# A chunked attention feeding a mixture of experts: the dense network moved wholly into the attention loop, and expert slots of 128 neighbouring rows

## The chip, the cores and the metric

The kernel runs on one core of a Trainium2 chip. The core has a matrix engine (PE, whose weight loads are listed as PEld), a vector engine (DVE), an activation engine (ACT), a general engine (POOL) and a sync engine (SP, which only issues transfers). All of them share 16 DMA engines. The metric is the device time of one execution in microseconds, lower being better.

## The reference, cut to what matters

```python
# attention: B, H, S, D = 4, 8, 768, 64; chunks of 32 queries that see 16 keys
# to the left, their own 32, 8 to the right, and 8 memory keys
for c in range(S // 32):
    k_full = np.concatenate([mem_k, k[:, :, l_start:r_end]], axis=2)
    v_full = np.concatenate([mem_v, v[:, :, l_start:r_end]], axis=2)
    a = softmax(np.matmul(q_c, k_full.transpose(0, 1, 3, 2)) / sqrt(D))
    out[:, :, c_start:c_end] = np.matmul(a, v_full)
x = out.transpose(0, 2, 1, 3).reshape(3072, 512)

# one dense network and eight experts, 512 -> 512 -> 512
y_dense = np.maximum(x @ w1_dense, 0.0) @ w2_dense
logits = x @ w_gate
expert_idx = np.argmax(logits, axis=1)
gate_w = softmax(logits)[np.arange(N), expert_idx]
for e in range(8):
    mask = expert_idx == e
    y_moe[mask] = gate_w[mask, None] * (np.maximum(x[mask] @ w1[e], 0.0) @ w2[e])
return y_dense + y_moe
```

Every token goes through the dense network and through one expert, chosen by its logits. Which expert gets how many tokens is known only when all logits are there.

## The kernel before

The 3072 tokens are 24 tiles of 128. The work has two stages, and the order of the instructions on each engine is the order in which the program is written.

**Attention loop.** It has 29 turns, counted by `i`. In one turn different tiles are at different steps: tile `i` has its scores made, tile `i-1` is transposed (`turn`), tile `i-2` is multiplied with the values and normalised, tile `i-3` becomes the network's input (`keep_x`, `turn_x`), tile `i-4` goes through the gate. Every third turn a group of three tiles gets its experts and its rows in the sorted array (`choose`, `rank`, `place`). A tile's row is then written by an indirect DMA (`scatter`, seven turns behind) to `xs` in DRAM, where each expert has a region of its own. A row of `xs` is 514 words: 256 words of the token's input as bf16, 256 words of the dense hidden layer as bf16, the sum of the exponentials of its logits, and its token number.

Keys and queries of the next batch are transposed on PE during the loop (`transposes`, one `step` for the keys or for the queries of two heads). A turn runs one step at its head, and in some turns a second one at its end; `steps_at` says how many. A key step is followed by two copies on ACT, a query step by one.

The first layer of the dense network (`dense`) comes seven turns behind: four matmuls with the tile as stationary operand and 512 hidden units as moving ones, into the one PSUM buffer of pool `pf`, and an activation on ACT that scales the result by the sum of exponentials and puts it into the row.

**Tables.** After the last turn DVE works out, for each of up to 31 slots, its expert (`expi`) and, for each of its 128 lanes, which row of `xs` to fetch (`rowi`). A lane without a token fetches a row of zeros.

**Slots.** A slot is up to 128 tokens of one expert. `fetch` gathers its rows by an indirect DMA on POOL. `turn` transposes input and dense hidden layer on PE, and DVE and ACT copy them out of PSUM. `bring` reads the expert's number into a register of DVE and copies that expert's two weight matrices to a fixed place. `first` is the first layer, with a relu on ACT. `second` adds the dense second layer and the expert's second layer in one PSUM buffer. `send` divides by the sum on ACT, and an indirect DMA on POOL writes the rows to the output. For the tokens of this input 27 slots suffice; slots 27 to 30 stand behind a branch on the number of slots (`tc.If(count > NSURE)`), placed before the last seven slots, and `run` gives the order around it.

All weights are cast to bf16 on the way in by DMAs that POOL issues (`load_w`); `next_w` issues one more at the turns of `W_AT`, the last ones during the first slots.

Of the kernel before, what the change touches and what calls it, by code (L numbers as in the profile page):

```python
# [17 lines left out]
ENGINES = [mybir.EngineType.PE, mybir.EngineType.DVE, mybir.EngineType.Activation]  # L18
# [7 lines left out]
NT = B * TPB  # L26
# [10 lines left out]
NSURE = 27  # L37
NSPLIT = 20
XW = DM // 2
ROW = 2 * XW + 2  # L40
ZROW = E * CAP
NOWHERE = 1 << 20
GRP = 3
QKB = 5
NVB = 4
W_AT = (10, 13, 15, 16, 18, 19, 21, 22, 24, 25, 26, 27)
NXG = 5
# [3 lines left out]
def kernel(  # L51
# [19 lines left out]
    xs = nc.dram_tensor("xs", [E * CAP + 1, ROW], I32, kind="Internal").ap()  # L71
# [14 lines left out]
    w_todo = [(E, 1)] + [(e, half) for e in range(E) for half in range(2)]  # L86
# [12 lines left out]
    zrow = const.tile([1, ROW], F32, name="zrow")  # L99
    rowi = const.tile([128, NSLOT], I32, name="rowi")  # L100
    expi = const.tile([128, NSLOT], I32, name="expi")
    nsl = const.tile([128, 1], I32, name="nsl")
# [8 lines left out]
    def constants():  # L111
        nc.vector.memset(ones, 1.0)
        nc.vector.memset(oh_sum, 0.0)
        nc.vector.memset(zrow, 0.0)
        nc.vector.memset(zrow[:, ROW - 2:ROW - 1], 1.0)
        nc.vector.memset(zrow[:, ROW - 1:ROW].bitcast(I32), NOWHERE)
        nc.sync.dma_start(xs[ZROW:ZROW + 1, :], zrow.bitcast(I32))
        for e in range(E):
            nc.gpsimd.memset(prio[:, e:e + 1], float(E - e))
            nc.gpsimd.memset(ecap[:, :, e:e + 1], float(e * CAP // 128))  # L120
        nc.gpsimd.iota(tok, [[128, NT]], base=0, channel_multiplier=1)
        nc.gpsimd.affine_select(upper, ones, pattern=[[1, 128]], base=0,
                                channel_multiplier=-1, compare_op=ALU.is_gt, fill=0.0)

    def table_constants():
        nc.gpsimd.iota(thr_i, [[128, NT]], base=0, channel_multiplier=0)
        nc.gpsimd.iota(lane_i, [[0, 1]], base=0, channel_multiplier=1)
        nc.gpsimd.iota(slot_i, [[1, NSLOT]], base=0, channel_multiplier=0)
# [7 lines left out]
    with ExitStack() as one:  # L136
# [138 lines left out]
        def attention(g, qT, kbd):  # L275
# [68 lines left out]
            def turn_x():  # L344
# [5 lines left out]
                xT = work.tile([128, DT, 128], BF16, tag="xT", name="xT", bufs=5)  # L350
# [9 lines left out]
            def dense():  # L360
                ph = pf.tile([128, F], F32, tag="ph", name="ph")
                for d in range(DT):
                    nc.tensor.matmul(ph, st["xT"][:, d, :], wall[:, E, d, :],  # L363
                                     start=(d == 0), stop=(d == DT - 1))
                nc.scalar.activation(st["row"][:, XW:2 * XW].bitcast(BF16), ph, AF.Relu,
                                     scale=st["grp"]["gt"][:, st["u"], 0:1])

            return {"scores": scores, "exp": expo, "turn": turn, "values": values, "norm": norm,
                    "keep_x": keep_x, "turn_x": turn_x, "gate": gate, "dense": dense}

        scatters = []
# [48 lines left out]
        def scatter(g):  # L420
# [5 lines left out]
                row.bitcast(I32), None, bounds_check=E * CAP - 1, oob_is_err=False)  # L426
            for o in scatters:
                tc.declare_no_dep(i.ins, o.ins, reason="different rows of xs")
# [27 lines left out]
        LAG_X, LAG_G, LAG_D = 3, 4, 7  # L456
        for i in range(NT + LAG_G + 1):
# [24 lines left out]
            if i == 2:  # L482
                load_w(E, 0)
                table_constants()
            if i in W_AT:
                next_w()
            if i % 2 == 0:
                load_v(i // 2 + 2)
# [25 lines left out]
            do("norm", 2)  # L514
            do("exp", 0)
# [13 lines left out]
            if i >= LAG_D:  # L529
                scatter(i - LAG_D)  # L530
        for g in range(NT + LAG_G + 1 - LAG_D, NT):
# [19 lines left out]
        nc.vector.tensor_copy(nsl, pin[:, E - 1:E])  # L551
# [9 lines left out]
        nc.vector.tensor_tensor(done, sw, ew(pin), ALU.is_ge)  # L561
        ex = tmp([128, NSLOT], "exq")
        nc.vector.reduce_sum(ex, done, axis=AX.X)
        nc.vector.tensor_scalar(expi, ex, float(E - 1), None, ALU.min)
        mine = wide_t[0][:, NSLOT * E:2 * NSLOT * E].rearrange("p (s e) -> p s e", e=E)
        nc.vector.tensor_tensor(mine, sw, ew(pex), ALU.is_ge)
# [7 lines left out]

        fr = tmp([128, NSLOT], "fr")
        nc.vector.tensor_tensor(fr, slot, st, ALU.subtract)
        nc.vector.tensor_scalar(fr, fr, 128.0, lane, op0=ALU.mult, op1=ALU.add)
        ok = tmp([128, NSLOT], "ok")
        nc.vector.tensor_tensor(ok, ce, fr, ALU.is_gt)
        nc.vector.scalar_tensor_tensor(fr, ex, float(CAP), fr, op0=ALU.mult, op1=ALU.add)  # L580
        nc.vector.scalar_tensor_tensor(fr, fr, float(-ZROW), ok, op0=ALU.add, op1=ALU.mult)
        nc.vector.tensor_scalar(rowi, fr, float(ZROW), None, ALU.add)

    with ExitStack() as two:
# [5 lines left out]
        xgs, xts, hs, copied = {}, {}, {}, {}  # L590
        own = [""]
        sent = []

        def fetch(j):
            xg = w3.tile([128, ROW], F32, tag="xg" + own[0], name="xg", bufs=NXG)
            nc.gpsimd.indirect_dma_start(  # L596
                xg.bitcast(I32), None, xs[:, :],
                bass.IndirectOffsetOnAxis(ap=rowi[:, j:j + 1], axis=0),
                bounds_check=ZROW, oob_is_err=True)
            xgs[j] = xg  # L600

        def turn(j):
            xb = xgs[j][:, :2 * XW].bitcast(BF16)
            xt = pt.tile([128, DT + FT, 128], BF16, tag="xt", name="xt")
            for d in range(DT + FT):
                nc.tensor.transpose(xt[:, d, :], xb[:, 128 * d:128 * d + 128], ident)  # L606
            xT = w3.tile([128, DT + FT, 128], BF16, tag="xT" + own[0], name="xT", bufs=2)
            nc.vector.tensor_copy(xT[:, :DT], xt[:, :DT])  # L608
            nc.scalar.copy(xT[:, DT:], xt[:, DT:])  # L609
            xts[j] = xT  # L610

        def bring(j):
            n = min(j + 1, E)
            ev = nc.vector.value_load(expi[:1, j:j + 1], min_val=0, max_val=n - 1)
            wa = w2.tile([128, DT, 512], BF16, tag="wa" + own[0], name="wa")
            wb = w2.tile([128, FT, 512], BF16, tag="wb" + own[0], name="wb")
            nc.vector.tensor_copy(  # L617
                wa, wall[:, :n][:, bass.ds(ev, 1), :DT].rearrange("p a t m -> p (a t) m"))
            nc.vector.tensor_copy(
                wb, wall[:, :n][:, bass.ds(ev, 1), DT:].rearrange("p a t m -> p (a t) m"))  # L620
            copied[j] = (wa, wb)

        def first(j):
            w, xT = copied[j][0], xts[j]
# [5 lines left out]
            h = w2.tile([128, FT, 128], BF16, tag="h", name="h")  # L630
# [3 lines left out]
        def second(j, dense):  # L634
            if dense:
                hs[j, "py"] = pf.tile([128, DM], F32, tag="py", name="py")
            py = hs[j, "py"]
            for f in range(FT):
                if dense:
                    nc.tensor.matmul(py, xts[j][:, DT + f, :], wall[:, E, DT + f, :],  # L640
                                     start=(f == 0), stop=False)
                else:
                    nc.tensor.matmul(py, hs[j][:, f, :], copied[j][1][:, f, :],  # L643
                                     start=False, stop=(f == FT - 1))

        def send(j, o=None, then=True):
            gw = w3.tile([128, 1], F32, tag="gw", name="gw")
            nc.vector.reciprocal(gw, xgs[j][:, ROW - 2:ROW - 1])  # L648
            if o is None:
                o = w3.tile([128, DM], F32, tag="o", name="o")  # L650
            nc.scalar.activation(o, hs[j, "py"], AF.Copy, scale=gw)  # L651
            if then:
                put(j, o)

        def put(j, o):
            i = nc.gpsimd.indirect_dma_start(  # L656
                out[:, :],
# [80 lines left out]
```

## Time and profile before

| | |
|---|---|
| three runs | 287.6, 291.04 and 290.42 us; median 290.42 us |
| the profiled execution | 287.78 us, its span 286.1 us |
| mean granted TensorE clock | 0.921 |
| PE busy | 219.7 us (77%) |
| PEld busy | 163.6 us (57%) |
| DVE busy | 173.0 us (60%) |
| ACT busy | 140.9 us (49%) |
| POOL busy | 190.5 us (67%) |
| DMA moved | 45.15 MB, mean 158 GB/s |

The span runs from the first to the last instruction; the device time is a little longer. A share is an average over stages with different limits. In the rows of a group stand line, engine, operation, output and inputs, sizes and count, then busy time and the mean of one in ns, then idle time of the engine just before and what ended it. In the rows of a timeline stand start, length, engine, line and operation, and in brackets the idle time before and what ended it. Matmuls are pipelined, so their lengths overlap and starts are the better measure.

### The profile page before, as it was taken

Reading aid. Unit: us, or ns where it says so; the run is one execution under the profiler, and the core shown is the slowest. Engines: PE = TensorE matmul, PEld = TensorE weight load, DVE = VectorE, ACT = ScalarE, POOL = GpSimd, SP = SyncE. Lnnn points to the kernel's source line nnn. Section 1 sums busy time; section 2 is a strip of 40 time slices with the busy share of each in tenths; the row PEclk is TensorE's granted clock in tenths of the full one; section 3 lists DMA queues with packets and bytes.
Section 4 is the critical chain, followed back from the end, with each engine's and each line's share of the span. In section 5 each row is a group of like instructions: output and inputs, shape, how many; then the busy total and the mean of one; then the engine's idle time right before and its main releaser. Section 6 shows DMA issues by size and latency. Waiting matters only on the chain. (4 is left out here: it accounts for less than half of the span.)

```text
span 286.1 us, 9435 instructions
## 1 busy us (share of the span) xinstructions
PE 219.7 (77%) x3770; PEld 163.6 (57%) x3804; DVE 173.0 (60%) x384; ACT 140.9 (49%) x230; POOL 190.5 (67%) x274
## 2 busy tenths in 40 slices
PE   2435759999879969998997202997999999865691
PEld 1324658877767857867775002664666667534460
DVE  5586356888768967988974711464556656552230
ACT  2434446776976767653553200353546656441341
POOL 8864034599958984885879807365676877887732
PEclk9999977999999997999999855797999999995979
DMA  6999546599998999699969995994455555454231
GB/s 88 179 200 172 109 84 93 101 174 166 170 234 134 212 218 221 96 210 223 200 129 177 204 165 123 193 230 141 139 158 158 183 153 173 152 162 131 84 112 60
DMA packets 54368, 45.15 MB, mean 158 GB/s; under 512 B 30319, under 2 KB 49263, under 8 KB 54322
## 3 DMA queue, kind: packets, MB, share of 16 engines
q0 software_dynamic: 25376, 36.54, 62.1%
q1 hardware_dynamic: 28946, 7.98, 15.2%
q8 instruction: 31, 0.51, 0.8%
q14 instruction: 15, 0.12, 0.1%
HBM read 46.05 MB, written 14.44 MB: 211 GB/s over the span
## 5 line engine op out<-in xcount | busy, mean ns | idle before, releaser
L596 POOL DMA_INDIRECT xg<-xs,rowi x31 | 36.6, 1180 | 24.3 <-issue 13.1
L609 ACT COPY xT<-xt 128x512 bf16<-128x512 bf16 x27 | 15.8, 586 | 59.9 <-DVE xT L608 59.9
L608 DVE COPY xT<-xt 128x512 bf16<-128x512 bf16 x27 | 11.5, 425 | 50.6 <-PE xt L606 50.6
L656 POOL DMA_INDIRECT out_dram<-o,xg x27 | 28.1, 1039 | 18.7 <-ACT o L651 9.0
L606 PE MATMUL xt<-ident,xg 128*128 128x128 bf16 x216 | 18.2, 233 | 25.6 <-DMA xg<-xs,rowi 25.6
L628 PEld LDWEIGHTS <-wa 128*128 128x128 bf16 x432 | 29.2, 105 | 9.0 <-issue 2.3
L606 PEld LDWEIGHTS <-xg 128*128 128x128 bf16 x216 | 15.0, 104 | 33.8 <-DMA xg<-xs,rowi 29.4
L424 POOL DMA_INDIRECT xs<-row,si x24 | 29.6, 1233 | 6.8 <-POOL row L423 6.5
L628 PE MATMUL ph<-xT,wa 128*128 128x128 bf16 x432 | 31.5, 231 | 1.5 <-ACTq L698 1.0
L351 POOL CAST xT<-x 128x512 bf16<-128x512 f32 x24 | 15.0, 626 | 25.0 <-ACT x L349 21.7
L643 PE MATMUL py<-wb,h 128*128 128x512 bf16 x108 | 30.8, 412 | 0.0
L357 PEld LDWEIGHTS pg<-wgate,x 128*128 128x128 f32 x192 | 26.1, 199 | 5.9 <-ACT qT L257 2.4
L322 PE MATMUL xp<-vw,aT 64*32 64x65 f32 x1536 | 25.6, 233 | 4.9 <-DMA vw<-mtpl 3.0
L223 DVE COPY vw<-vw 24x1820 f32<-24x1820 f32 x24 | 27.5, 1147 | 2.5 <-DMA vw<-in_v_dram 1.8
L363 PE MATMUL ph<-wall,xT 128*128 128x512 bf16 x76 | 23.5, 390 | 5.8 <-issue 2.1
L341 POOL CAST row<-xn 128x512 bf16<-128x512 f32 x24 | 19.5, 814 | 11.6 <-DVE xn L334 11.4
L617 DVE COPY wa<-wall 128x2048 bf16 (+1 forms) x27 | 20.4, 755 | 11.3 <-DVE gw L648 7.6
L305 ACT ACTIVATE a<-a 128x512 f32<-128x512 f32 x24 | 15.1, 630 | 24.0 <-DVE a L300 22.5
L640 PE MATMUL py<-wall,xT 128*128 128x512 bf16 x94 | 25.6, 388 | 0.9 <-issue 0.2
L357 PE MATMUL pg<-wgate,x 128*128 128x8 f32 x192 | 24.4, 253 | 2.3 <-DMA wgate<-in_moe_w_gate_dram 2.3
L322 PEld LDWEIGHTS xp<-vw,aT 64*32 64x32 f32 x1536 | 19.2, 109 | 11.7 <-issue 5.6
L265 ACT COPY kbd<-tp 64x768 bf16<-64x768 bf16 x28 | 22.1, 790 | 3.4 <-PE tp L252 3.2
(122 smaller groups left out, 449.4 us busy)
## 6 DMA issues: line engine op xcount, KB each, us to landing
wall<-in_moe_w_dram POOLq DMA_DIRECT2D x16, 512.0 KB, 9.2
vw<-in_v_dram SPq DMA_DIRECT2D x64, 64.0 KB
kb<-in_k_dram POOLq DMA_DIRECT2D x16, 192.0 KB, 6.0
qb<-in_q_dram POOLq DMA_DIRECT2D x16, 192.0 KB, 6.9
vw<-in_v_dram SPq DMA_DIRECT2D x32, 56.0 KB
vw<-mtpl SPq DMA_DIRECT2D x24, 65.0 KB
wall<-in_moe_w_dense_dram POOLq DMA_DIRECT2D x2, 512.0 KB, 8.5
xg<-xs,rowi POOLq DMA_INDIRECT x31, 4.2
```

The lines of the kernel that those rows point to most:

```text
L223: nc.vector.tensor_copy(vw[r + 32:r + 56, :PC - 1], vw[r:r + 24, 1:])
L265: nc.scalar.copy(dst, tv[r])
L322: nc.tensor.matmul(xp[32 * cc:32 * cc + 32, par, (D + 1) * hp:(D + 1) * (hp + 1)], st["aT"][r, hp, 32 * cc:32 * cc + 32], vw[r, 4 * (g % 2 ...
L357: nc.tensor.matmul(grp["pg"][:, u, :], st["x32"][:, d, :], wgate[:, d, :], start=(d == 0), stop=(d == DT - 1))
L363: nc.tensor.matmul(ph, st["xT"][:, d, :], wall[:, E, d, :], start=(d == 0), stop=(d == DT - 1))
L424: i = nc.gpsimd.indirect_dma_start(xs[:, :], bass.IndirectOffsetOnAxis(ap=grp["si"][:, u:u + 1], axis=0), row.bitcast(I32), None, bounds_c ...
L596: nc.gpsimd.indirect_dma_start(xg.bitcast(I32), None, xs[:, :], bass.IndirectOffsetOnAxis(ap=rowi[:, j:j + 1], axis=0), bounds_check=ZROW, ...
L606: nc.tensor.transpose(xt[:, d, :], xb[:, 128 * d:128 * d + 128], ident)
L628: nc.tensor.matmul(ph[:, f, :], w[:, d, 128 * f:128 * f + 128], xT[:, d, :], start=(d == 0), stop=(d == DT - 1))
L640: nc.tensor.matmul(py, xts[j][:, DT + f, :], wall[:, E, DT + f, :], start=(f == 0), stop=False)
L643: nc.tensor.matmul(py, hs[j][:, f, :], copied[j][1][:, f, :], start=False, stop=(f == FT - 1))
L656: i = nc.gpsimd.indirect_dma_start(out[:, :], bass.IndirectOffsetOnAxis(ap=xgs.pop(j)[:, ROW - 1:ROW].bitcast(I32), axis=0), o, None, boun ...
```

## The change

The dense network is computed wholly in the attention loop. `dense1` makes the hidden layer in the transposed form, with sixteen matmuls of 128 columns, and ACT applies the relu (`hd`). `dense2`, at the end of the same turn, multiplies with the second weights. `keep_y`, at the head of the next turn, copies the fp32 result into the row. The row grows to 770 words, and tile `i-5` is the one that is worked on. Both PSUM results use the one buffer of pool `pf`.

In `xs` each expert's region begins with 128 filler rows, which SP writes in turns 3 to 10 (`front`) from an entry of `wall` that DVE fills with ones. A slot then fetches 128 neighbouring rows, from a start that SP reads into a register; an expert's last slot starts earlier, so that it ends with its last row, and what it holds twice or too much is sent nowhere (`past`).

In the slots the dense parts are gone. `bring` copies the first weights only; for the second ones PE reads the expert's number into a register and addresses `wall` by it. ACT alone copies the transposed input. DVE makes the output with one multiply-add. The second layer of a slot comes one slot after its first. The branch is gone, and all 31 slots run. The buffers of keys and queries go from five to four, those of `xg` from five to six, and the second dense weights are loaded at turn 4 instead of 10.

```diff
-ROW = 2 * XW + 2
+ROW = XW + DM + 2
+REG = CAP + 128
-QKB = 5
+QKB = 4
-NXG = 5
+NXG = 6
...
+        nc.vector.memset(wall[:, E - 1], 1.0)
...
+    def front(e):
+        i = nc.sync.dma_start(
+            xs[REG * e:REG * e + 128, :],
+            wall[:, E - 1].rearrange("p t m -> p (t m)")[:, :2 * ROW].bitcast(I32))
...
-            def dense():
-                ph = pf.tile([128, F], F32, tag="ph", name="ph")
-                for d in range(DT):
-                    nc.tensor.matmul(ph, st["xT"][:, d, :], wall[:, E, d, :],
-                                     start=(d == 0), stop=(d == DT - 1))
-                nc.scalar.activation(st["row"][:, XW:2 * XW].bitcast(BF16), ph, AF.Relu,
-                                     scale=st["grp"]["gt"][:, st["u"], 0:1])
+            def dense1():
+                ph = pf.tile([128, FT, 128], F32, tag="pf", name="ph")
+                for f in range(FT):
+                    for d in range(DT):
+                        nc.tensor.matmul(ph[:, f, :], wall[:, E, d, 128 * f:128 * f + 128],
+                                         st["xT"][:, d, :], start=(d == 0), stop=(d == DT - 1))
+                hd = work.tile([128, FT, 128], BF16, tag="hd", name="hd")
+                nc.scalar.activation(hd, ph, AF.Relu)
+                st["hd"] = hd
+
+            def dense2():
+                py = pf.tile([128, DM], F32, tag="pf", name="py")
+                for f in range(FT):
+                    nc.tensor.matmul(py, st["hd"][:, f, :], wall[:, E, DT + f, :],
+                                     start=(f == 0), stop=(f == FT - 1))
+                st["py"] = py
+
+            def keep_y():
+                nc.scalar.copy(st["row"][:, XW:XW + DM], st["py"])
...
-        LAG_X, LAG_G, LAG_D = 3, 4, 7
+        LAG_X, LAG_G, LAG_D, LAG_S = 3, 4, 5, 7
...
             if i > 0 and steps and steps_at[i % TPB] > 0:
                 steps.pop(0)()
...
-            if i < NT + LAG_G:
-                do("dense", LAG_D)
-            else:
-                for g in range(i - LAG_D, NT):
-                    parts[g]["dense"]()
+            do("keep_y", LAG_D + 1)
+            do("dense1", LAG_D)
             do("gate", LAG_G)
...
             do("values", 2)
             do("norm", 2)
+            do("dense2", LAG_D)
             do("exp", 0)
...
         def fetch(j):
-            xg = w3.tile([128, ROW], F32, tag="xg" + own[0], name="xg", bufs=NXG)
-            nc.gpsimd.indirect_dma_start(
-                xg.bitcast(I32), None, xs[:, :],
-                bass.IndirectOffsetOnAxis(ap=rowi[:, j:j + 1], axis=0),
-                bounds_check=ZROW, oob_is_err=True)
+            at = nc.sync.value_load(rowi[:1, j:j + 1], min_val=0, max_val=E * REG - 128)
+            xg = w3.tile([128, ROW], F32, tag="xg", name="xg", bufs=NXG)
+            nc.sync.dma_start(xg.bitcast(I32), xs[bass.ds(at, 128), :])
...
-            nc.vector.tensor_copy(
-                wb, wall[:, :n][:, bass.ds(ev, 1), DT:].rearrange("p a t m -> p (a t) m"))
...
+        def second(j):
+            n = min(j + 1, E)
+            ev = nc.tensor.value_load(expi[:1, j:j + 1], min_val=0, max_val=n - 1)
+            w = wall[:, :n][:, bass.ds(ev, 1), DT:].rearrange("p a t m -> p (a t) m")
+            py = pf.tile([128, DM], F32, tag="py", name="py")
+            for f in range(FT):
+                nc.tensor.matmul(py, hs[j][:, f, :], w[:, f, :],
+                                 start=(f == 0), stop=(f == FT - 1))
+            send(j, py)
...
+            nc.vector.scalar_tensor_tensor(o, py, gw, xg[:, XW:XW + DM],
+                                           op0=ALU.mult, op1=ALU.add)
...
-        with tc.If(count > NSURE):
...
+        for j in range(NSLOT + 1):
+            next_w()
+            bring(j + 1)
+            if j < NSLOT:
+                first(j)
+            turn(j + 2)
+            if j:
+                second(j - 1)
+                fetch(j - 1 + NXG)
```

More of the change, by code (lines that the diff above doesn't have):

```diff
@@ L662, in put @@
             sent.append(i)
-        def run(js, then=(), os=None):
-            todo = js + list(then)
-            for n, j in enumerate(js):
-                next_w()
-                if n + 1 < len(todo):
-                    bring(todo[n + 1])
-                first(j)
-                second(j, True)
-                if n + 1 < len(todo):
-                    turn(todo[n + 1])
-                second(j, False)
-                send(j, os and os[j], os is None)
-                if os is None and n + NXG - 1 < len(todo):
-                    fetch(todo[n + NXG - 1])
-        front, rest = list(range(NSPLIT)), list(range(NSPLIT, NSURE))
-        more = list(range(NSURE, NSLOT))
-        for j in front[:NXG - 1]:
+        for j in range(NXG):
             fetch(j)
```

140 lines of the change are left out of this document (56 added, 84 removed).

## The prediction, made before the changed kernel ran

> **What bounds the kernel now.** I read the busy time by stage first (columns: stretch, its length, busy time and instruction count of each engine, granted TensorE clock, DMA share, GB/s).
>
> ```profile
> 55.60:142.79 87.19, 79.48 (x1957) 64.04 (x1972) 72.42 (x151) 56.95 (x95) 69.00 (x107) 0.98 1.04 186
> 161.00:176.30 15.30, 0.01 (x1) 0.02 (x2) 3.23 (x10) 0.47 (x1) 5.96 (x7) 0.55 0.80 153
> 176.30:245.00 68.70, 65.50 (x636) 45.07 (x647) 37.36 (x79) 35.07 (x59) 46.25 (x43) 0.93 0.64 170
> 245.00:286.10 41.10, 25.87 (x216) 16.78 (x218) 13.27 (x27) 13.29 (x22) 25.47 (x26) 0.87 0.37 116
> ```
>
> There are three stages. In the attention loop PE works 79.48 of 87.19 us, so a microsecond given to PE there lengthens the run, and 7.7 us of idle is all that can absorb it. Then PE stands for 15 us at the seam. The expert slots are PE-bound again until 245, and the last 41 us, around the branch, leave PE idle for over a third. Next I read PE's order in one attention turn (start, length, engine, line; starts count, since lengths contain the pipeline's drain).
>
> ```profile
> 91.83 1.04 PE L363 MATMUL ph<-wall,xT 128*128 128x512 bf16 x3
> 92.70 0.95 PE L357 MATMUL pg<-wgate,x 128*128 128x8 f32 x8
> ...
> 95.06 0.86 PE L322 MATMUL xp<-vw,aT 64*32 64x65 f32 x64
> 95.85 0.53 PE L252 MATMUL tp<-ident,qb 128*64 128x128 bf16 x12
> 96.31 1.04 PE L363 MATMUL ph<-wall,xT 128*128 128x512 bf16 x3
> ```
>
> From one dense to the next is 4.48 us, of which the old dense takes 0.87 and a key or query transpose 0.46. The same view for one expert slot:
>
> ```profile
> 218.01 1.06 PE L628 MATMUL ph<-xT,wa 128*128 128x128 bf16 x16
> 218.90 1.03 PE L640 MATMUL py<-wall,xT 128*128 128x512 bf16 x4
> 219.76 0.61 PE L606 MATMUL xt<-ident,xg 128*128 128x128 bf16 x8
> 220.21 1.03 PE L643 MATMUL py<-wb,h 128*128 128x512 bf16 x4
> 221.07 1.06 PE L628 MATMUL ph<-xT,wa 128*128 128x128 bf16 x16
> ```
>
> A slot is 3.06 us, all PE: 0.89 first layer, 0.86 dense second layer, 0.45 transposes, 0.86 expert second layer.
>
> **Part 1, dense into attention: PE's work.** Sixteen 128-wide matmuls (0.89) replace four 512-wide (0.87), and four 512-wide more (0.86) follow: +0.88 us a tile, 24 tiles, **+21.1 us**. ACT gains one copy a tile.
>
> **Part 2, dense into attention: a new wait.** Both results now use the one PSUM buffer of pool `pf`. So `dense1` of a tile cannot start until ACT has run `keep_y` of the tile before. The price of such a handoff shows where the old kernel runs three denses in a row:
>
> ```profile
> 157.93 1.02 PE L363 MATMUL ph<-wall,xT 128*128 128x512 bf16 x4 [0.78 <-ACT row L365]
> 157.19 0.69 ACT L365 ACTIVATE row<-ph,gt 128x512 bf16<-128x512 f32 x1 [2.07 <-PE ph L363]
> ```
>
> PE idles 0.78 for a 0.69 activation, so both semaphores together cost 0.1; with the drain, the next start is some 0.94 late. Worse is the place. In the changed kernel's built order ACT's queue at the head of a turn is: copies of the key or query transposes, then `keep_y`, then the new relu. PE does the transposes and stands at `dense1`; gate, turn, scores and values are queued behind it. The old dense waited only for an activation of the turn before. ACT's prices:
>
> ```profile
> 71.25 1.58 ACT L265 COPY kbd<-tp 64x768 bf16<-64x768 bf16 x2
> 75.19 0.78 ACT L257 COPY qT<-tp 128x768 bf16<-128x768 bf16 x1
> 75.86 1.60 ACT L265 COPY kbd<-tp 64x768 bf16<-64x768 bf16 x2
> 95.35 0.60 ACT L349 COPY x<-xtp 128x512 f32<-128x512 f32 x1
> ```
>
> `keep_y` is a copy of the last kind, 0.60. After a key transpose PE waits 1.6 + 0.6 + 0.1 = 2.3 us; after a query 0.8 + 0.6 + 0.1 = 1.5; after a query at the end of one turn and keys at the start of the next, 0.35 more than keys alone (0.8 of copy less the 0.46 that PE transposes), 2.65; with none, 0.85. `steps_at` gives the counts for turns 6 to 28: five keys (6, 8, 10, 14, 16), four queries, three doubles (11, 12, 17), one query left over (18), ten bare: 11.5 + 6.0 + 7.95 + 1.5 + 8.5 = **35.4 us**.
>
> What it absorbs: idle that already stands before the old dense, and part of the rest.
>
> ```profile
> L363 PE MATMUL ph<-wall,xT 128*128 128x512 bf16 x52 | 16.9, 396 | 4.0 <-issue 2.1 <-POOL row L423 1.2 <-PE tp L252 0.2
> ```
>
> That is −4.0 (it falls in turns that now wait anyway), half of the other 3.7, −1.9, and −3.0 at the end, where three denses with two handoffs in the last turn become one. Bounds for these three: 0 to −10.7.
>
> **Part 3, the clock.** A wait of 2 us has a second price here:
>
> ```profile
> 106.13 0.28 PE L289 MATMUL sc<-kbd,qT 128*32 128x112 bf16 x7 [1.99 <-issue]
> 106.00:108.00 2.00, 1.87 (x83) 1.52 (x85) 1.51 (x3) 0.62 (x2) 0.55 (x2) 0.95 1.23 264
> 108.00:110.00 2.00, 1.67 (x24) 1.28 (x22) 1.86 (x4) 2.00 (x3) 1.72 (x3) 0.50 1.11 212
> 110.00:112.00 2.00, 2.00 (x13) 1.63 (x12) 1.15 (x2) 1.53 (x3) 0.70 (x2) 0.69 1.19 203
> 82.61 0.81 PE L363 MATMUL ph<-wall,xT 128*128 128x512 bf16 x3 [1.47 <-issue]
> 80.00:90.00 10.00, 8.37 (x211) 7.10 (x204) 7.73 (x20) 7.29 (x13) 6.21 (x10) 1.00 1.02 214
> ```
>
> After 1.99 us of idle the granted clock was 0.50 for about 3.3 us (0.05 x 2 + 0.5 x 2 + 0.31 x 2 = 1.7 us of work lost); after 1.47 it stayed 1.00. Eight waits are 2.3 or longer: 0 to 13.6 us. I take 8, since part of a slow stretch falls into the next wait. [...]
>
> Attention: 21.1 + 35.4 − 8.9 + 8 = **+55.6 us** (46 to 70). Three edits I cost at nothing. The eight `front` writes on SP, 0.39 MB each, need 10 us of DMA at the full rate of part 5; they are spread over turns 3 to 10, which PE makes over 20 us longer. The fill of one `wall` entry on DVE at turn 0 is of the size of
>
> ```profile
> 2.31 2.70 DVE L439 MEMSET kbd<- 128x3168 uint32 x1 [0.61 <-issue]
> ```
>
> and lies in the start-up, where PE waits for loads; uncovered it would cost its 3 us. Fewer key buffers hold loads back on POOL until a transpose of an earlier turn, still some three turns ahead of their use.
>
> **Part 4, the seam.** The old gather stands on POOL until the scatters have landed:
>
> ```profile
> 162.55 0.98 POOL L424 DMA_INDIRECT xs<-row,si  x1 [0.28 <-POOL row L423]
> 172.80 1.10 POOL L596 DMA_INDIRECT xg<-xs,rowi  x1 [8.46 <-issue]
> 176.29 1.03 PE L606 MATMUL xt<-ident,xg 128*128 128x128 bf16 x8 [15.54 <-DMA xg<-xs,rowi]
> xs<-row,si POOLq DMA_INDIRECT x24, 6.2
> ```
>
> Rows grow from 2056 to 3080 bytes, which slows scatter and gather; slower turns leave less weight traffic ahead of the scatters, which may then land in the usual 6.2 us rather than 9.3. But POOL no longer waits, so four weight loads start at once and run against the first gathers. I take −1 (−5 to +4).
>
> **Part 5, the slots.** PE loses 0.86 and half of 0.45: 3.06 − 1.08 = 1.98 us. DVE loses `wb` and `xT`, and gains the final multiply-add:
>
> ```profile
> 215.17 0.69 DVE L617 COPY wa<-wall 128x2048 bf16 x1 [0.33 <-DVE gw L648]
> 217.75 0.15 DVE L648 RECIPROCAL gw<-xg 128x1 f32<-128x1 f32 x1
> DVE wa L617 <- DVE gw L648: 7.6, 21, 0.7
> 79.94 0.69 DVE L300 TENSOR_TENSOR a<-sc,mx 128x512 f32<-128x512 f32 x1
> L614 DVEq TENSOR_LOAD <-expi x27: 299/304/656, 162.9 to 272.1; - x27
> 210.00:220.00 10.00, 9.95 (x103) 6.56 (x103) 5.91 (x13) 5.71 (x10) 7.39 (x7) 1.00 0.52 166
> ```
>
> `wa` 0.69, two small operations 0.15 each, the multiply-add like L300 0.69, the register load 7.6/21 = 0.36: 2.04 us. DMA: a slot moves 128 x (3080 + 2048) bytes = 656 KB; 166 GB/s at a share of 0.52 is 319 GB/s full, so 2.06 us. PE's own register load, 0.30 for the read alone, may or may not hide. Three limits within 0.1 us of each other do not run at their floor, and a gather has only about two slots to land after its buffer is free: I take 2.4 us a slot (2.06 to 2.9). All 31 slots run, 27 before. Fill is two transposes and a first layer, 1.4 us; the drain is as now:
>
> ```profile
> 279.08 1.04 PE L643 MATMUL py<-wb,h 128*128 128x512 bf16 x4
> ```
>
> from 280.1 to the span's end at 286.1, 6.0 us. So 31 x 2.4 + 7.4 = 81.8 us, against 286.1 − 176.3 = 109.8 now: **−28 us** (−38.5 to −12.5). That holds the branch's fallout, since the slots run straight through.
>
> **Sum.** 286.1 + 55.6 − 1 − 28 = 312.7 us of span; the profiled run took 287.78, 1.7 above its span, so 314.4, say **314**. That run is 0.9% below the median shown, 290.42. About 2% is what a measurement here can tell from no change.
>
> **The rivals.**
> - *The handoff is covered.* If something else holds PE back before `dense1`, ACT is done by then and the 35.4 and the clock vanish: 286.1 + 21.1 − 4.9 − 1 − 28 + 1.7 = 275 us, faster. For it: the slot stage surely shrinks, and DMA is at a share of 1.04 in the loop. Against: PE has 7.7 us of idle there in all. It turns to slower once over 13 us of waits remain, and is within 2% from 7 to 19.
> - *The clock stays up.* The waits do not trip it: 306 us. For it: 1.47 us did not; against: 1.99 did. [...]
> - *The clock is tripped everywhere.* Query waits count too, on top of all key waits: 13 x 1.7 = 22 instead of 8, 328 us. Against: the 1.00 from 80 to 90.
> - *The slots starve.* Gathers or the address reads on PE hold a slot to 2.9: 330 us. For it: larger gathers; against: six buffers instead of five.
>
> **How the numbers follow.** Forecast 0.45; covered handoff 0.13, of which 0.04 ends within 2%; clock up 0.20; clock down 0.11; starved slots 0.11. The range runs from clock up with fast slots (306 − 9 = 297) to starved slots with a little of the clock case (333); what lies below is the covered handoff, and about 0.06 above. Faster 0.09, same 0.04, slower 0.87.
>
> **What would show it.** In attention, PE should idle before the first LDWEIGHTS of `dense1` with ACT's `row<-py` copy as releaser: about 2.3, 1.5, 0.85 us by kind of turn, 30 us or more in all; a turn with keys should take 7.5 to 8 us. Half-clock stretches should follow key turns. First transposes of the slots at about 231 us, then one slot every 2.4. I am wrong if those waits sum to under 13 us, or if slots need over 2.9.

## The result and the profile after

The changed kernel took 331.06 us (median of four runs, 326.83 to 333.35) against 290.34 for the kernel before: 1.131 times as long, 95% interval 1.119 to 1.144. Some runs of most kernels here come out one to six per cent longer than the fastest of the same kernel, so a ratio with an interval is one of the undisturbed runs alone (here 326.83 and 329.47 us against the four of before), while the medians and ranges are of all runs. The profiled execution took 332.65 us, its span is 330.8 us, its mean granted clock 0.862 (0.921 before).

From the page of the changed kernel: span, busy time and granted clock in 40 slices, in tenths of full speed; the last row is the clock of the kernel before.

```profile
span 330.8 us, 10323 instructions
PE 240.4 (73%) x4068; PEld 186.0 (56%) x4068; DVE 174.8 (53%) x397; ACT 140.4 (42%) x235; POOL 156.6 (47%) x239
PEclk9999678799965896675789999999556999999996
...
PEclk9999977999999997999999855797999999995979
```

PE's share of busy time fell from 77% to 73% although it was given work, and the row of clock digits has holes down to 0.5, from the fifth slice to the 21st, up to the end of the keys' and queries' transposes; before, the digits fell only at the start-up's end, once in the loop, at the seam and a little in the slots.

PE's waits by releaser (total, number, longest) and PE's timeline at `dense1` (in brackets the wait ahead of it):

```profile
PE ph L368 <- ACT row L382: 32.5, 22, 2.7
...
55.15 1.65 PE L368 MATMUL ph<-xT,wall 128*128 128x128 bf16 x16 [2.65 <-ACT row L382]
65.18 1.07 PE L368 MATMUL ph<-xT,wall 128*128 128x128 bf16 x16 [1.38 <-ACT row L382]
73.15 1.07 PE L368 MATMUL ph<-xT,wall 128*128 128x128 bf16 x16 [2.29 <-ACT row L382]
99.73 1.84 PE L368 MATMUL ph<-xT,wall 128*128 128x128 bf16 x16 [2.66 <-ACT row L382]
138.84 1.07 PE L368 MATMUL ph<-xT,wall 128*128 128x128 bf16 x16 [1.39 <-ACT row L382]
176.85 0.34 PE L368 MATMUL ph<-xT,wall 128*128 128x128 bf16 x3 [0.64 <-ACT row L382]
```

(The last row is from a narrow stretch, hence three of the sixteen matmuls.) The wait stands where it was forecast, with the copy `row<-py` as releaser, and close to the forecast sizes: 2.3 after keys, 1.38 after queries, 2.66 after both, 0.64 to 0.68 in a bare turn.

The seam: the last scatter, the four weight loads behind it on POOL, the first fetch on SP and the first transposes on PE. Then the first layers of two neighbouring slots.

```profile
230.02 0.99 POOL L438 DMA_INDIRECT xs<-row,si  x1 [0.28 <-POOL row L437]
231.00 3.10 POOL L80 DMA_DIRECT2D wall<-in_moe_w_dram  x4
240.47 6.07 SPq L616 DMA_DIRECT2D xg<-xs  x6
246.32 0.61 PE L625 MATMUL xt<-ident,xg 128*128 128x128 bf16 x4 [17.71 <-DMA xg<-xs]
...
253.98 1.06 PE L645 MATMUL ph<-xT,wa 128*128 128x128 bf16 x16
...
255.96 1.06 PE L645 MATMUL ph<-xT,wa 128*128 128x128 bf16 x16
```

The fetch is issued only 9.5 us after the last scatter, and its rows are there 5.9 us later. A slot alone is 1.98 us of PE (253.98 to 255.96); the first layers of slots 0 and 30 start at 248.56 and 320.08, so a slot is 2.38 us on the mean.

By stage, before against after: loop to the end of the last scatter's issue 163.5 and 231.0 (+67.5); from there to the first transposes 12.8 and 15.3 (+2.5); from there to the end 109.8 and 84.5 (−25.3). The sum is +44.7, the difference of the spans.

**Where the clock went.** The granted clock of the changed kernel's loop falls and rises on a fixed grid. These windows have been cut along it, 3.41 us each (columns: stretch, length, busy time and count of PE, PEld, DVE, ACT, POOL, granted clock, DMA share, GB/s):

```profile
52.09:55.50 3.41, 0.76 (x22) 0.60 (x17) 0.97 (x1) 2.87 (x4) 1.45 (x1) 0.99 0.49 88
55.50:58.92 3.42, 3.42 (x24) 3.42 (x22) 0.40 (x3) 0.63 (x2) 0.00 (x0) 0.50 0.75 216
58.92:62.33 3.41, 3.41 (x92) 2.50 (x91) 2.21 (x7) 1.91 (x4) 0.60 (x1) 0.51 0.65 160
62.33:65.74 3.41, 2.03 (x33) 1.45 (x32) 3.10 (x8) 1.36 (x3) 2.41 (x4) 1.00 0.62 134
65.74:69.16 3.42, 3.42 (x106) 3.12 (x105) 1.24 (x3) 1.69 (x3) 0.78 (x3) 1.00 1.04 202
69.16:72.57 3.41, 1.70 (x41) 0.78 (x25) 2.28 (x4) 2.36 (x5) 2.96 (x5) 1.00 1.10 194
72.57:75.98 3.41, 2.83 (x49) 2.71 (x50) 0.00 (x0) 1.46 (x3) 2.40 (x6) 1.00 1.03 204
...
96.46:99.88 3.42, 0.76 (x25) 0.60 (x20) 0.99 (x3) 2.87 (x4) 2.24 (x4) 0.99 1.21 288
99.88:103.29 3.41, 3.41 (x26) 3.41 (x25) 0.00 (x0) 0.60 (x1) 0.00 (x0) 0.50 1.05 188
103.29:106.70 3.41, 3.41 (x92) 2.81 (x91) 1.49 (x3) 1.38 (x3) 0.20 (x1) 0.51 0.05 16
```

A window is wholly at 1.00 or wholly at 0.50. The window in which a wait of 2.65 lies whole (52.09, PE busy 0.76) is followed by two slow ones; the wait of 2.29 at 73.15 falls across a border (PE busy 1.70 and 2.83 in the two windows) and costs no clock. Between 54 and 172 us eight slow stretches begin, at 55.5, 89.5, 99.75, 113.5, 127.0, 140.75, 147.5 and 161.25, and they are one, two or three windows long: 55 us in all, so 27 us of PE's time are lost. Seven of them begin in or right behind one of the eight waits of 2.3 us or longer, and one, at 140.75, follows the query wait before 138.84; the other four query waits cost no clock.

### The profile page after: what moved, and what is told of

The parts are those of the page before. It is cut to its first block, busy times and chain, and to the rows that moved or that the text cites. A ratio compares the mean times of both kernels' runs of the same rounds, so it can differ in the third digit from the quotient of the medians.

```text
span 330.8 us, 10323 instructions
## 1 busy us (share of the span) xinstructions
PE 240.4 (73%) x4068; PEld 186.0 (56%) x4068; DVE 174.8 (53%) x397; ACT 140.4 (42%) x235; POOL 156.6 (47%) x239
## 4 chain that ended last, share of the span: by engine, by line
PE 54%; issue 11%; ACT 11%; DMA 10%; SPq 3%; POOL 2%; DVE 1%; POOLq 0%; ACTq 0%; DVEq 0%
PE ph L368 8%; PE py L657 7%; PE pg L361 7%; PE py L377 6%; PE ph L645 6%; PE xp L326 6%; PE xtp L351 5%; PE ap L314 4%; ACT kbd L269 4%; ACT row L382 3%; DMA xs<-row,si 3%; PE sc L293 2%; ACT qT L261 2%; DMA mtpl<-in_mem_v_dram 2%; PE tp L256 2%
## 5 line engine op out<-in xcount | busy, mean ns | idle before, releaser
L671 POOL DMA_INDIRECT out_dram<-o,to x31 | 38.7, 1248 | 52.5 <-DVE o L669 51.3
L368 PE MATMUL ph<-xT,wall 128*128 128x128 bf16 x384 | 29.2, 237 | 32.5 <-ACT row L382 32.5
L368 PEld LDWEIGHTS <-wall 128*128 128x128 bf16 x384 | 24.7, 106 | 38.0 <-ACT row L382 37.9
L302 DVE TENSOR_REDUCE mx<-sc 128x8 f32<-128x512 f32 x24 | 16.6, 691 | 39.2 <-PE sc L293 38.9
L657 PE MATMUL py<-wall,h 128*128 (+1 forms) x124 | 32.0, 381 | 6.8 <-ACT h L648 4.3
L648 ACT ACTIVATE h<-ph 128x512 bf16<-128x512 f32 x31 | 18.5, 597 | 39.7 <-PE ph L645 39.7
L669 DVE SCALAR_TENSOR_TENSOR o<-py,gw,xg 128x512 f32<-128x512 f32 x31 | 23.3, 750 | 21.7 <-PE py L657 21.3
L377 PE MATMUL py<-wall,hd 128*128 128x512 bf16 x96 | 27.7, 416 | 0.7 <-ACT hd L371 0.7
L371 ACT ACTIVATE hd<-ph 128x512 bf16<-128x512 f32 x24 | 14.3, 597 | 31.6 <-PE ph L368 31.6
L314 PE MATMUL ap<-identf,a 128*128 128x128 f32 x96 | 19.8, 342 | 7.6 <-ACT a L309 7.6
```

Source lines behind the costliest of these rows:

```text
L314: nc.tensor.transpose(ap[:, hp, :], st["a"][:, 2 * hp:2 * hp + 2, :], identf)
L368: nc.tensor.matmul(ph[:, f, :], wall[:, E, d, 128 * f:128 * f + 128], st["xT"][:, d, :], start=(d == 0), stop=(d == DT - 1))
L377: nc.tensor.matmul(py, st["hd"][:, f, :], wall[:, E, DT + f, :], start=(f == 0), stop=(f == FT - 1))
L657: nc.tensor.matmul(py, hs[j][:, f, :], w[:, f, :], start=(f == 0), stop=(f == FT - 1))
L669: nc.vector.scalar_tensor_tensor(o, py, gw, xg[:, XW:XW + DM], op0=ALU.mult, op1=ALU.add)
L671: i = nc.gpsimd.indirect_dma_start(out[:, :], bass.IndirectOffsetOnAxis(ap=to, axis=0), o, None, bounds_check=NT * 128 - 1, oob_is_err=False)
```

## The experiments

All kernels of one group below ran on one chip together with the kernel before, and the chips differ: before took 300.9 us (300.24 to 308.15) beside the first group, 305.5 (293.57 to 309.39) beside the second and 305.0 (298.27 to 312.19) beside the third. So ratios to that are compared, and absolute forecasts, made for the chip of the result, may be some per cent low. Where no interval stands, medians and ranges are given, and beside the ratio of the medians that of the lowest runs; the two can differ by several per cent.

### First group: is it the wait?

**two_banks**: the first dense layer gets a bank of the other pool.

```diff
-                ph = pf.tile([128, FT, 128], F32, tag="pf", name="ph")
+                ph = ps.tile([128, FT, 128], F32, tag="ps", name="ph")
```

> The hidden layer of dense1 goes into the rotating PSUM pool of four buffers; only dense2's result stays in the single one, so no matmul stands behind keep_y. Theory (the handoff wait, and the half clock that it trips): the 33 us of PE waits behind the row copy go to under 2, the granted clock is 1.00 through the loop, which gives back some 20 us more: 277 us, 271 to 285. Rival 1 (the waits count, the clock does not): 331 - 33 = 298. Rival 2 (the loop is long because of the added matmuls and copies, and the wait only shows where ACT or DVE is late; it comes back elsewhere): 320 or more.

Measured: 290.36 us (283.29 to 292.89), 0.965 of before by the medians, 0.944 by the lowest runs. One line of the kernel turns 1.13 into less than one. PE's waits and the clock:

```profile
PE xt L625 <- DMA xg<-xs: 19.3, 2, 18.1
PE xp L326 <- issue: 5.9, 5, 1.6
PE py L377 <- issue: 5.7, 17, 1.7
PE ph L368 <- issue: 2.7, 1, 2.7
PEclk9999969999989699999989999955589999999996
```

The wait behind the row copy is gone from the list; the first transposes start at 205.74 instead of 246.32, and the slots take 82.7 us as before (84.5). What stands in its place are stalls put down to "issue", the longest here, in a stretch in which the transfers' share is 1.08:

```profile
92.38 0.71 PE L368 MATMUL ph<-xT,wall 128*128 128x128 bf16 x5 [2.74 <-issue]
88.90:92.40 3.50, 0.76 (x14) 0.59 (x13) 0.58 (x1) 2.75 (x4) 1.32 (x2) 0.99 1.08 263
```

It lies within the sixteen matmuls of one `dense1`, and the trace names no other engine that ended it; this one, too, is followed by half clock (0.50 for the two windows from 92.40). The last section says where such stalls stand.

**keepy_early**: `keep_y` runs at the end of its own turn, behind `exp`, and no longer at the head of the next.

```diff
-            do("keep_y", LAG_D + 1)
...
             do("exp", 0)
+            do("keep_y", LAG_D)
...
-        parts[NT - 1]["keep_y"]()
```

> Same single PSUM buffer, but keep_y stands at the end of the turn, behind the exponential and ahead of all copies of key and query transposes. Theory (place in ACT's queue): the wait falls to about 0.85 us in the bare turns, 0.4 where one transpose lies between, 0 where two do: 12 us in all instead of 33, no wait reaches 2 us, clock 1.00: 290 us, 282 to 298. Rival 1 (no clock effect): 308. Rival 2 (it is the single buffer, whatever the place): waits as before, 325 or more.

Measured: 297.4 us (295.28 to 301.55), ratio 0.987, interval 0.976 to 0.997. The waits behind the copy, in all, number and longest:

```profile
PE ph L368 <- ACT row L382: 6.1, 13, 0.7
```

The one bank remains and its waits fall from 32.5 to 6.1 us. So the price came from what stands ahead of `keep_y` in ACT's queue, not from sharing as such.

**keys_split**: DVE makes the second of the two key copies in every batch, so that ACT has one less ahead of `keep_y`.

```diff
-                        if b == 0 and par:
+                        if par:
```

> Everything as in the changed kernel, but of the two copies behind a key transpose one goes to DVE in all batches, as in the first batch already. The wait in a key turn shrinks from 2.3 to about 1.6 us, in a double turn from 2.65 to about 1.9; that is 6 us in all. Theory (a wait of 2 us trips the half clock, one of 1.4 does not): the clock comes back in most of the loop, another 14 to 20 us: 308 us, 303 to 315. Rival (the clock has nothing to do with the length of the wait, or costs nothing): 6 us only, 325.

Measured: 307.39 us (307.1 to 314.03), ratio 1.022, interval 1.019 to 1.026.

```profile
PE ph L368 <- ACT row L382: 24.7, 21, 2.1
PEclk9999989999799799996999999995559999999996
```

7.8 us less of waits than in the changed kernel; the slow time in the loop is 13.7 us (four windows in three stretches) instead of 55. Most of what this edit brings is therefore clock, not wait. It brings more than forecast (308 us on the chip of the result would be 1.06 of before).

**weights_early**: all sixteen weight loads go into the loop, none behind the last scatter.

```diff
-W_AT = (10, 13, 15, 16, 18, 19, 21, 22, 24, 25, 26, 27)
+W_AT = (8, 9, 10, 11, 12, 13, 14, 15, 16, 17, 18, 19, 20, 21, 22, 23)
```

> All sixteen weight loads go at turns 8 to 23, none at turns 24 to 27 nor in the first slots. Theory (the last scatters and the first gathers stand behind or beside weight loads): from the end of the last scatter's issue to the first transpose of the slots 15.3 us become 9 to 10: 326 us, 322 to 329. Rival (landing of the scatters and of the first gather costs that much by itself): 331, the stretch 14 us or more.

Measured: 319.47 us (311.81 to 329.37), 1.062 of before by the medians, 1.039 by the lowest runs.

```profile
228.03 0.99 POOL L438 DMA_INDIRECT xs<-row,si  x1 [0.28 <-POOL row L437]
232.39 6.06 SPq L616 DMA_DIRECT2D xg<-xs  x6
235.75 0.61 PE L625 MATMUL xt<-ident,xg 128*128 128x128 bf16 x4 [9.12 <-DMA xg<-xs]
```

From the scatter's end to the first transposes 6.7 us instead of 15.3: the loads that POOL issues at once hold up the landing of the scatters (3.4 us instead of 9.5) and the first fetch (3.4 instead of 5.9). The time is below the forecast range, which counted the seam only: of the 11.2 us by which this span is shorter than the changed kernel's, the seam gives 8.6, and the ratio to before fell from 1.131 by more than twice the seam's share. Where the rest comes from is not shown; the number of half-rate windows in the loop differs between executions even of one kernel (16 in the changed kernel's trace, 12 in control's below), and the mean granted clock from 60 to 165 us is 0.78 in the changed kernel's trace and 0.82 here.

### Second group: wait or clock, and how much further?

**control**: the changed kernel unaltered.

> The changed kernel itself, beside the old one and the other kernels of this call on one chip. About 1.13 times the old one, by every theory.

Measured: 334.58 us (330.96 to 338.74), waits behind the row copy 34.4 us. The ratio to before is 1.095 by the medians and 1.127 by the lowest runs.

**busy_wait**: the changed kernel with idle matmuls ahead of `dense1`, into a bank of the other pool, as many as fill the wait. Nothing reads their result. In the edit `ended` says that a step stood at the end of the turn before.

```diff
+            fill = 6 if ended else 3
             if i > 0 and steps and steps_at[i % TPB] > 0:
+                fill = 6 if len(steps) % 2 else 11 if ended else 10
                 steps.pop(0)()
...
+            if i > LAG_D:
+                spin = ps.tile([128, 512], F32, tag="ps", name="spin")
+                for _ in range(fill):
+                    nc.tensor.matmul(spin, ident, wall[:, E, 0, :], start=True, stop=True)
             do("dense1", LAG_D)
```

> The changed kernel with idle matmuls, whose result nothing reads, put on PE ahead of dense1: ten of 512 columns in a turn with keys, eleven in a double, six with a query, three in a bare one, 0.215 us each, so that PE computes about as long as it would wait. The work and the waits of the rest stay. Theory (a wait of 2 us trips the half clock, which costs some 20 us): the clock stays at 1.00 through the loop and the kernel gets faster by doing more, by 10 to 22 us less a few us where the filling is longer than the wait: 0.94 to 0.97 of the control. Rival (the clock does not cost time, or falls for another reason): the same as the control or up to 10 us slower.

Measured: 310.45 us (308.72 to 311.55), 0.928 of control by the medians, 0.933 by the lowest runs, a little more than forecast. By turns these are 40 after keys (four turns of ten), 44 after both (four of eleven), 30 after queries and 30 in bare turns, 144 matmuls of 0.215 us or 31 us more for PE to do, and the kernel is 22 to 24 us faster. The granted clock of the control, then of this kernel:

```profile
PEclk9999659699797897579789999998557999999997
PEclk9999859999999999999999999996559999999998
```

Apart from start-up and seam there is no slow stretch left. The traces agree with the times: the last scatter's issue ends at 232.3 us in control and at 208.9 here, and up to there control is at half rate for 45 us more, which is 22 us lost. This prices the clock's term by itself: 22 to 24 us of the changed kernel's time.

**both**: two_banks and weights_early together.

> two_banks and weights_early together. Theory: the waits behind the row copy and their clock are gone, and the stretch from the last scatter's issue to the first transpose of the slots is 7 us instead of 18 as in two_banks alone: some 8 us less than two_banks, 0.94 of the old kernel. Rival (a shorter loop with sixteen weight loads in it is short of DMA, so that what the seam gives is lost in the loop): as two_banks, 0.965 of the old kernel.

Measured: 297.82 us (293.78 to 300.65), 0.975 of before by the medians and 1.001 by the lowest runs: no better than two_banks alone. From the last scatter's end (199.87) to the first transposes (206.84) are 7.0 us, so the seam's gain is there; the loop gave it back:

```profile
PE xp L326 <- DVE vw L230: 13.8, 5, 6.2
PE xp L326 <- issue: 7.5, 6, 2.4
116.00:126.00 10.00, 0.44 (x8) 0.20 (x8) 1.30 (x2) 0.00 (x0) 0.00 (x0) 0.63 1.19 218
```

For ten microseconds the engines hardly work while the transfers' share is 1.19; DVE, for whose copy of the values PE waits 13.8 us, itself waits 10.7 us for their loads ahead of that copy (`vw<-in_v_dram`). The rival held.

**one_of_four**: two_banks with one of the four matmuls of the second dense layer; three quarters of that layer's sum are left out.

```diff
-                for f in range(FT):
-                    nc.tensor.matmul(py, st["hd"][:, f, :], wall[:, E, DT + f, :],
-                                     start=(f == 0), stop=(f == FT - 1))
+                nc.tensor.matmul(py, st["hd"][:, 0, :], wall[:, E, DT, :],
+                                 start=True, stop=True)
```

> two_banks, but dense2 does one of its four matmuls only (three quarters of the dense second layer are left out). Theory (without the wait the loop is bound by PE, so the added matmuls cost their own time): 24 x 3 x 0.215 = 15.5 us less than two_banks. Rival (the loop without the wait is bound by transfers or by ACT and DVE): under 6 us less.

Measured: 286.39 us (283.58 to 294.34), 0.937 of before by the medians and 0.966 by the lowest runs, where two_banks stands at 0.965 and 0.944 on another chip. So the times do not decide. The traces say a little more: the last scatter's issue ends at 181.05 us here, and at 190.04, 188.94 and 185.38 in two_banks, two_27 and two_again, whose loops are the same. That is 4 to 9 us for 24 x 0.65 = 15.5 us of PE work taken away, so PE's work seems to be the bound of two_banks only for part of the loop. What bounds the rest was not tested.

### Third group: what is the best version, and how short a wait slows the clock?

**two_again**: two_banks once more, as the measure for the next two.

> The kernel of two_banks once more, on this chip, as the measure for the next two. Theory (the wait behind the row copy was the loss, the slots' saving is real): 0.95 to 0.98 of before here too, slots at 2.4 us. Rival (0.965 was that chip's state): 0.99 or more.

Measured: 288.86 us (288.3 to 296.81), ratio to before 0.957, interval 0.935 to 0.979. One bank more makes the change a gain.

**two_27**: two_banks with 27 slots.

```diff
+NRUN = 27
...
-        for j in range(NSLOT + 1):
+        for j in range(NRUN + 1):
```

> two_banks with 27 slots instead of 31, which is enough for this input's tokens and not for every input. Theory (a slot costs 2.4 us wherever it stands): 4 x 2.4 = 9.6 us under two_again. Rival (the last slots only fill the drain of transfers that would be waited for anyway): less than 5 us under it.

Measured: 282.55 us (276.61 to 286.47), 6.3 less than two_again by the medians and 11.7 by the lowest runs, which does not decide between the forecasts. In the traces the stage from the first transposes to the end is 84.1 us in two_again and 77.1 here, 7.0 for four slots, between the forecasts of 9.6 and of under 5. First and last first layer of two_again, then of this kernel:

```profile
204.47 1.91 PE L645 MATMUL ph<-xT,wa 128*128 128x128 bf16 x16
275.74 1.06 PE L645 MATMUL ph<-xT,wa 128*128 128x128 bf16 x16
```

```profile
207.47 1.91 PE L646 MATMUL ph<-xT,wa 128*128 128x128 bf16 x16
272.02 1.06 PE L646 MATMUL ph<-xT,wa 128*128 128x128 bf16 x16
```

71.27 / 30 = 2.38 us a slot against 64.55 / 26 = 2.48. A slot is not a fixed price: by the stages of these two traces the last four come at 1.75 us each.

**two_spread**: two_banks with all sixteen loads in the loop, but late.

```diff
-W_AT = (10, 13, 15, 16, 18, 19, 21, 22, 24, 25, 26, 27)
+W_AT = (10, 12, 13, 14, 15, 16, 17, 18, 19, 20, 21, 22, 23, 24, 25, 26)
```

> two_banks with all sixteen weight loads in the loop, but late: turns 10 and 12 to 26 instead of 8 to 23, when the keys' and queries' loads end. Theory (the stretch between loop and slots shrinks to 8 us from 15, and the bare turns have free transfers, so that the loop loses 3 at most): 4 to 6 us under two_again. Rival (the loop is short of transfers until the end, and loads at the end hold the scatters back): within 3 us of two_again, or above it.

Measured: 289.02 us (284.19 to 293.63), the same as two_again by the medians and 4.1 us less by the lowest runs. The stretch between scatter and transposes is 9.4 us (190.86 to 200.25) against 16.9 there (185.38 to 202.29), but the loop ends 5.5 us later than there, and 1.9 later than in two_27, whose loop is that of two_again. So the loop pays for part of what the seam gains, and how much is left is open: neither forecast is refuted.

**long_only**: busy_wait with the idle matmuls only where the wait is 2.3 us or longer.

```diff
-            if i > LAG_D:
+            if i > LAG_D and fill > 6:
```

> busy_wait with the idle matmuls only where the wait was 2.3 us or longer (after keys, ten or eleven of them); the waits of 1.4 us after queries and 0.7 us in bare turns stay idle. Theory (only the long waits halve the clock): granted clock 1.00 through the attention loop as in busy_wait, and within 1.5% of its 1.016 of before. Rival (the short waits trip it too, once the long ones no longer hide that): stretches of 0.50 behind query waits, and 1.04 of before or more.

Measured: 314.34 us (312.96 to 316.15), ratio 1.043, interval 1.025 to 1.061. The times do not decide, since busy_wait's 1.016 is a ratio of medians and its lowest runs give 1.052. The clock does, and my theory fell. Two of its waits behind a query, then the window of this kernel's grid in which each lies (the first but for its last 0.09 us), with the two that follow the second:

```profile
61.43 1.07 PE L368 MATMUL ph<-xT,wall 128*128 128x128 bf16 x16 [1.39 <-ACT row L382]
110.71 1.07 PE L368 MATMUL ph<-xT,wall 128*128 128x128 bf16 x16 [1.38 <-ACT row L382]
57.92:61.34 3.42, 2.08 (x74) 1.37 (x54) 3.22 (x8) 2.31 (x4) 2.35 (x4) 1.00 0.50 106
...
109.12:112.54 3.42, 2.04 (x33) 1.88 (x28) 1.99 (x7) 1.88 (x3) 2.97 (x4) 1.00 0.19 63
112.54:115.95 3.41, 3.41 (x89) 2.82 (x92) 1.38 (x2) 1.28 (x3) 2.12 (x5) 0.50 0.84 127
115.95:119.36 3.41, 3.36 (x52) 1.62 (x36) 2.00 (x3) 1.55 (x3) 3.12 (x5) 1.00 1.23 199
```

Three of the five query waits (76.56, 110.71, 127.61) are followed by one slow window each, 1.7 us lost apiece; the wait of 1.39 at 61.43, as long, by none. So the length of the wait doesn't decide, and PE's busy time in the window, 2.08 against 2.04, doesn't either; what differs is the time of weight loads beside it, 1.37 against 1.88 us. The last section comes back to this.

## Why the prediction was right, step by step

The time fell into the range and on the forecast side, 17 us above the value given, with the clock's term far too small and two others short. That it still fell into the range is in part luck: the upper end, 333, was set for starved slots, which did not come.

- **Part 2, the wait: as forecast.** 2.3, 1.5, 2.65 and 0.85 were forecast by kind of turn; 2.3, 1.38, 2.66 and 0.66 were measured, 32.5 us in all where 35.4 stood. The count by kind was off by one, since a query step ends turn 5 and makes turn 6 a double; the sum hardly changes. That it is ACT's order and not the bank as such is shown by keepy_early (waits 6.1 us); that it decides the sign, by two_banks and two_again (0.957 of before, interval 0.935 to 0.979).
- **Part 3, the clock: the step that failed.** "0.50 for about 3.3 us", eight times. There were eight slow stretches, but only two lasted one window of 3.4; four lasted two and two lasted three. 55 us at half rate cost 27 us of PE's time, 41 us in control's execution cost 20, and busy_wait gained 22 to 24, where I took 8. That the number of stretches came out at the eight of the long waits is chance: one long wait was spared and one query wait was not. I had read the length off the one stretch that the trace of before has in its loop, behind a wait followed by dense work. Behind these waits comes a `dense1` of small matmuls, whose weight loads fill the window (3.42 of 3.42 us in the row at 55.50, at 0.50), and the window after it was still at 0.51. What keeps it there wasn't tried. The rival with the clock tripped everywhere, at 328 us, was the nearest, for the wrong reason: query waits can count (long_only, where its price of 1.7 held), but in the changed kernel only one of five did, and a stretch cost 3.4 on the mean.
- **The clock stays up.** This rival (306 us) is refuted. In the changed kernel's loop every change of clock lies on the grid of 3.41 us, and windows with PE busy 0.76 and 2.03 us of it were followed by 0.50; without these slow stretches busy_wait is 22 to 24 us faster than control.
- **Part 1, PE's work: not refuted, not measured by itself.** The traces of one_of_four and two_banks suggest that 15.5 us of it are worth 4 to 9 once the waits are gone, so adding the work in full was probably too dear for a kernel without the wait. In the changed kernel the loop grew by 67.5 us, with 21.1 of work, 32.5 of waits and 26 of additional clock loss (1.7 was lost before); the difference, −12, is what was absorbed or is counted twice in these sums, where I took −8.9.
- **Part 4, the seam: the sign failed.** +2.5 instead of −1. The four loads, which I had named as the risk, are the cause: without them 6.7 us instead of 15.3 (weights_early). The larger rows did not show in the scatters' landing: its median is 6.2 us before and 5.8 after.
- **Part 5, the slots: right.** 2.38 us a slot against 2.4, above the three limits of 1.98, 2.04 and 2.06, and −25.3 instead of −28 us for the stage.
- **The covered handoff** at 275 us needed the waits to be hidden. They weren't, and where they were taken away, two_again gave 0.957 of before, interval 0.935 to 0.979, with which 275 / 290.4 = 0.947 agrees. In the loop of two_banks PE still waits 15.3 us, in 24 pieces, that are put down to "issue"; the last section comes back to them.

## What to carry to other kernels

Before two results share a buffer, look up what stands ahead of its reader in that engine's queue: here the price was that queue, 32.5 us of waits, and a copy issued earlier (6.1 us left) or a second bank (none left) took it away. Count a wait of the matrix engine twice, once in its own length (32.5 us here) and once in the clock of the windows behind it (27 us of PE's time here); if it can't be removed, matmuls without a use ahead of it can pay (22 to 24 us of 335 here). A gain at one stage that is bought with transfers moved into a stage that is short of them can be no gain (both at 0.975 of before, two_banks alone at 0.965), although the same move was one while the loop was longer (weights_early, 1.062 where the changed kernel had 1.131).

## What the runs showed of the hardware

- The granted clock changed only on a grid of 3.41 us, in all eight loops that were cut along it (before, the changed kernel, control, two_banks, two_again, both, keys_split and long_only): each window was at 0.99 to 1.00 or at 0.50 to 0.51. A slow stretch was one to four windows long there (four in both from 118.5).
- PE busy 2.03 of 3.42 us at 137.42 of the changed kernel was followed by half rate, while 1.70 of 3.41 at 69.16 was not. From 45 to 200 us of these eight traces, all 17 full-rate windows with PE busy up to 1.4 us were followed by 0.50, of the 51 from 1.49 to 2.41 us 16 were, and of the 223 above that none.

```profile
137.42:140.84 3.42, 2.03 (x28) 2.00 (x27) 0.66 (x3) 1.88 (x3) 1.17 (x2) 0.99 0.85 148
140.84:144.25 3.41, 3.41 (x92) 2.71 (x90) 2.25 (x7) 1.75 (x4) 0.30 (x1) 0.51 0.91 140
```

- In the first of these two rows weight loads are busy 2.00 us beside PE's 2.03, at 69.16 only 0.78 beside 1.70. Of 24 full-rate windows of these traces with PE busy 1.9 to 2.15 us, the seven with loads of 1.8 us or more were all followed by 0.50, of the other 17 one was (both at 84.39, PE 2.10 and loads 1.50, while the changed kernel's window at 62.33, PE 2.03 and loads 1.45, was followed by 1.00). Of 34 half-rate windows with PE busy throughout, the nine with loads of 2.9 us or more were all followed by another slow one, of the other 25 three were. No run varied the loads alone, so what decides is not shown.
- The waits of PE in two_banks's loop that are put down to "issue" are 5.9 us before the values' matmuls (5 waits), 5.7 before `dense2` (17), 2.7 in `dense1` (1) and 1.0 before the scores (1). Three of them, 1.02 us before 78.09, 2.74 before 92.38 and 1.21 before 116.93, stand 253 and 505 matmuls apart. In the trace of before the three such waits of 0.45 us or longer in the loop, 1.47 before 82.61, 1.99 before 106.13 (from which the price of the clock was read) and 0.45 before 127.75, stand 502 and 501 recorded matmuls apart. Each of the latter three ends 2.6 to 3.1 us after the start of a packet (79.49, 103.17 and 125.13) of the queue that its page lists so:

```profile
q8 instruction: 31, 0.51, 0.8%
```

- No run changed anything about these packets, so that PE waits for them is not shown.
